# Mapped queries stored by the projections, a third bank for some maxima scores, two changed orders and a normalisation on ScalarE, in an infini-attention block with a gated feed-forward layer

## The chip, the cores and the metric

The kernel runs on one core of a Trainium2 chip. The metric is the device time of one execution in microseconds (us). Several engines of the core work side by side, each on its own sequence of instructions: TensorE (PE; its weight loads, PEld, are shown apart), VectorE (DVE), ScalarE (ACT), GpSimd (POOL), and SyncE (SP), which only issues transfers here. PSUM is the memory that TensorE writes its results into; the kernel divides it into banks of 128 x 512 fp32. SBUF is the memory for everything else on the core.

## The reference

A transformer block over 2048 tokens of width 576: attention with a compressive memory, then a gated feed-forward layer of width 4608, each after a layer normalisation that is scaled and shifted by a vector computed from a condition `c`. The attention has 32 heads of width 18 and goes through four segments of 512 tokens. Within a segment it is causal softmax attention; a memory matrix `M` and a normaliser `z` per head carry the segments before.

```python
mod = (_silu(c) @ w_mod).reshape(c.shape[0], 6, 1, -1)      # sa, ca, ga, sb, cb, gb
h = _layernorm(x) * (1 + ca) + sa
# attention: q, k, v = h @ wq, h @ wk, h @ wv, split in heads and segments
phi = lambda t: jnp.where(t > 0, t + 1.0, jnp.exp(t))
for s in range(N):
    logits = jnp.einsum("bhqd,bhkd->bhqk", qs, ks) * scale + mask
    p = _softmax(logits, axis=-1)
    a_dot = jnp.einsum("bhqk,bhkd->bhqd", p, vs)
    pq = phi(qs)
    num = jnp.einsum("bhld,bhde->bhle", pq, M)
    den = jnp.einsum("bhld,bhd->bhl", pq, z)[..., None] + 1e-6
    outs.append(g * num / den + (1.0 - g) * a_dot)
    pk = phi(ks)
    M = M + jnp.einsum("bhld,bhle->bhde", pk, vs)
    z = z + jnp.einsum("bhld->bhd", pk)
x = x + ga * (o @ wo)
h = _layernorm(x) * (1 + cb) + sb
x = x + gb * ((_silu(h @ w_gate) * (h @ w_up)) @ w_down)
```

All data is fp32.

## The kernel before

**Precision.** Products of fp32 matrices are made as three products of a high and a low part (`ah`, `al`, `dh`, `dl`, `wh`, `wl` and so on are such parts): high times high, high times low, low times high. A high part is made by a ScalarE copy that rounds, the low part by a VectorE subtraction.

**Projections.** Segment by segment (the loop `for s in range(NSEG)`), `proj(s, t)` makes nine tiles t of 128 rows of the q and k projections, transposed, 14 matmuls each (`mm14`, L100) into one of three PSUM banks tagged "p". Two ScalarE copies take a tile out of its bank (`fh`, `f`), a VectorE subtraction makes `fl`, and SP's queue stores the parts in DRAM (`kD`, `qD`). The order of the tiles is `QKORD`, 0 to 8: tiles 0 to 3 and half of 4 are k, the other half of 4 and tiles 5 to 8 are q. For segments above 0 the plain q rows are stored as well, in `qF`. `phi_k` maps the keys (a transpose by TensorE, minimum with 0, exponential, combine: L440 to L442), `vproj` makes v, `mem` adds to the memory matrix `mbd`. During segments 1 to 3 the generator `early()` makes the maxima of the first two units of the attention.

**Attention.** A unit u is four heads of one segment, so a segment s has eight units q = 0 to 7 and there are 32 in all. Every unit is a row of eleven steps, in an order written out by hand (`tc.manual_schedule()` keeps the instructions of each engine in the order of the program). In a step:
- `p2_step` makes the scores of unit u, keys by queries, in one of two PSUM banks tagged "s2" (L609), and ScalarE takes their exponential out of the bank (L612). GpSimd cuts off the part above the diagonal.
- `p1_step` makes scores of unit u + 2, queries by keys, in one of two banks "s1" (L184), of which VectorE takes the row maxima (L189). These are folded into the operand of that unit's `p2_step` through an extra row of `qst`. `p1_seq(u)` runs through all four row tiles of a unit.
- The events of the table `PAT` follow: one row of eleven strings for even and one for odd units of the first and of the second half of a segment. V: the product with v (L629); E, c, d: its way out of PSUM and its normalisation; A to D and G: reading the memory for the next segment with the mapped queries `pq` (L809); M, R, S, T, X, Z: the output projection of a segment that is done, whose accumulator is a single PSUM bank with the tag "w". Its first use is in unit 9 (`w = u - 9`). l, p, x: the layer normalisation behind it.
- The events f, g and h make the mapped queries of the next segment, row block t in the segment's unit q = t: f (one unit ahead; the call `event("f", -1)` before the loop makes the very first) loads the plain rows from `qF`; g runs three ScalarE passes, relu(-q), exp of its negative, relu(q) (L787 to L789); h adds two of them on GpSimd into `pq`.

The loads of a unit's operands (`load_stack`, four transfers) are issued three units ahead on SP's queue.

**Output projection of segment 3.** It runs after the attention, 8 groups of four steps n = 0 to 31. A group accumulates 14 matmuls (`wo_m`, L738) in one of two banks, and `wo_x` (L743) adds the result to the residual. The tuples `SS`, `HH` and `WW` say at which n the work for the following stage is woven in: sums of weight blocks (`sum_o`, L1161), sums of the operand (`y_here`), and with `WW` the first five weight pieces of the first pair (`prep_w`: a cast by ScalarE, L1175, and a subtraction by VectorE, L1176; with the first two also `prep_r`, the remainder rows).

**Feed-forward layer.** Tokens in two halves t, hidden columns in 18 pairs p. Gate (z = 0) and up (z = 1) are made with seven block products each, in the manner of Strassen and Winograd: `step(z, m)` runs product m with seven matmuls (`prod`, L1211) into a bank "A" (two of them), "B" or "C". Products 1, 6, 7 and 4 use A: 1 and 7 are added to by 6 and 4, and between the two a copy is taken (`copy_t`, L1240: `tb` after 6, `tc` after 7, in the very first set also `cu` after 1). `step` keeps the current A bank in `B["A"]`. The order of a pair's 14 products is `ZM`; the first set of all is taken in the order of indices `PRIME`. In the first half the generator `prep2` prepares the operand of the second half. It begins with the layer normalisation of five row tiles `xl` (L1078 to L1094), whose subtraction and scaling is the VectorE operation at L1092; the other tiles are normalised during the attention by GpSimd (L769) and ScalarE (L770).

Of the kernel before, what the change touches and what calls it, by code (L numbers as in the profile page):

```python
# [46 lines left out]
WW = (9, 11, 14, 18, 26)  # L47
# [7 lines left out]
PRIME = (0, 1, 3, 2, 5, 4) + tuple(range(6, 14))  # L55
# [5 lines left out]
PAT = (["", "M0", "V2 V3 m E D", "n", "M1 Q G", "c", "M2 d", "V0 g", "h A0 q M3 R S X", "T Y Z B0", "A1 P V1 z B1 f C"],  # L61
# [12 lines left out]
def block(ctx: ExitStack, tc: tile.TileContext, x, wqk, wv, wo, beta, wgu, wd, c, w_mod, wm01, out):  # L74
# [83 lines left out]
    mcol, pmt, mrow = {}, {}, {}  # L158

# [14 lines left out]
    def p1_step(u, b, i, ps, jp, jb):  # L174
# [6 lines left out]
        for h0 in range(0, 4, per):  # L181
            bank = ps.tile([P, L], F32, tag="s1", name="s1", bufs=S1B)
            for h in range(h0, h0 + per):
                nc.tensor.matmul(bank[:, n * (h - h0):n * (h - h0) + n],  # L184
                                 lhsT=qst[b][0:108, h, 128 * i:128 * i + 128],
                                 rhs=kst[b][0:108, h // 2, 0:n], start=True, stop=True)
            for h in range(h0, h0 + per):
                junk = jp.tile([P, L], BF16, tag="junk", name="junk", bufs=jb)
                nc.vector.tensor_tensor_reduce(junk[:, :n], bank[:, n * (h - h0):n * (h - h0) + n], tri[:, L - n:],  # L189
                                               1.0, -3e38, op0=ALU.add, op1=ALU.max, accum_out=mx[:, h, i:i + 1])  # L190
            if h0 + per < 4:
                yield
# [54 lines left out]
    with ExitStack() as p1:  # L247
# [211 lines left out]
        def proj(s, t):  # L459
# [16 lines left out]
            if q1 > 0:  # L476
# [4 lines left out]
                if s > 0:  # L481
                    nc.sync.dma_start(qF[s][q0:q1, :], f[r:])
# [108 lines left out]
    def p1_seq(u):  # L591
        if NE <= u < NU:
            for i in range(4):
                yield from p1_step(u, u % NB, 3 - i, ps, wk, 4)
# [182 lines left out]
    def phi_q(s, t):  # L777
        r = 64 if t == 0 else 0
        q0 = 0 if t == 0 else 64 + 128 * (t - 1)
        f = wk.tile([P, L], F32, tag="qf", name="qf", bufs=2)  # L780
        nc.sync.dma_start(f[r:], qF[s][q0:q0 + P - r, :])
        return f

    def phi_q2(s, t, f):
        r = 64 if t == 0 else 0
        e = wk.tile([P, L], F32, tag="qe", name="qe", bufs=1)
        nc.scalar.activation(e[r:], f[r:], AF.Relu, scale=-1.0)  # L787
        nc.scalar.activation(e[r:], e[r:], AF.Exp, scale=-1.0)
        nc.scalar.activation(f[r:], f[r:], AF.Relu)  # L789
        return e  # L790

    def phi_q3(s, t, f, e):
# [4 lines left out]
        nc.gpsimd.tensor_tensor(pqs[s][r:, t, :], e[r:], f[r:], op=ALU.add)  # L797
# [54 lines left out]
    def event(ev, u):  # L852
# [206 lines left out]
    def prep2(x2p):  # L1059
# [19 lines left out]
        for sn, i in ((2, 3), (3, 0), (3, 1), (3, 2), (3, 3)):  # L1079
# [10 lines left out]
            nc.gpsimd.tensor_tensor(rs, rs, mhalf[:, :1], op=ALU.pow)  # L1090
            yield
            nc.vector.tensor_scalar(xl, xl, mv[:, 0:1], rs[:, 0:1], op0=ALU.subtract, op1=ALU.mult)  # L1092
# [151 lines left out]
    def step(z, m):  # L1244
        prime = "set" not in B
        if m == 1:
            B["A"] = ps.tile([P, L], F32, tag="A", name="A", bufs=2)
# [3 lines left out]
        bank = B["B" if m == 2 else "C" if m in (5, 3) else "A"]  # L1251
# [104 lines left out]
    with tc.manual_schedule():  # L1356
# [4 lines left out]
        event("f", -1)  # L1361
# [291 lines left out]
```

## Time and profile before

| | us |
|---|---|
| device time, median of 3 runs | 1878.56 |
| lowest and highest run | 1877.34, 1879.14 |
| profiled execution, device time | 1879.11 |
| its span in the trace | 1877.4 |
| projections, from the start to the first step of the attention | 0 to 235 |
| attention, unit by unit | 235 to 594 |
| output projection of segment 3 | 594 to 612 |
| feed-forward layer | 612 to 1877 |

The borders of the stages are rounded to the microsecond. How the views of the profile are read:
- A row of busy time gives the engine, its busy us, the share of the span, and the number of instructions. Durations of matmuls overlap.
- A row of a group of instructions gives the line, the engine, the operation, output <- inputs with their shape, and the count; then busy us and mean ns of one; then the engine's idle time just before them and what ended most of it.
- A row of the timeline gives the start, the duration, the instruction, and in brackets how long the engine had been idle and what released it.
- A row of the waits gives the waiting instruction, what it waited for, and total us, times, and the longest.
- The chain of waits is followed back from the last instruction of a stretch, at each step to what released it, or else to the instruction before it on its engine.

### The profile page before, as it was taken

What the parts mean: (1) busy time and instruction counts of PE and PEld (TensorE: products, weight loads), DVE (VectorE), ACT (ScalarE), POOL (GpSimd) and SP (SyncE); (2) the same over time, 40 slices, a digit from 0 to 9 for tenths busy, and PEclk for the clock granted to TensorE, in tenths of its full rate; (3) what the DMA queues carried; (4) which work ended last, traced back from release to release, by engine and by line L of the source; (5) the groups of instructions that cost most, each with busy time, mean ns of one, the idle gap of its engine ahead of it and who ended that gap; (6) DMA issues with size and microseconds to landing.
All of it is one profiled execution on the core that took longest, in us unless ns stands there. A gap on an engine that the chain in (4) does not pass through costs nothing.

```text
span 1877.4 us, 30668 instructions
## 1 busy us (share of the span) xinstructions
PE 1855.3 (99%) x10933; PEld 1562.4 (83%) x10933; DVE 1487.8 (79%) x3282; ACT 978.4 (52%) x2138; POOL 507.8 (27%) x696
## 2 busy tenths in 40 slices
PE   8999999999999999999999999999999999999999
PEld 5988856777767788888888888888888888888888
DVE  7555278888886888888888888758888888888886
ACT  7433387768676534454544544434454454544442
POOL 2010046455565154454554454300000000000000
PEclk9999999999999999999999999999999999999999
DMA  8766644447655745555545534485333432333331
GB/s 299 248 224 239 221 146 146 144 141 197 170 161 211 248 160 193 164 169 186 186 153 169 168 125 150 151 286 186 104 102 100 125 103 87 115 104 124 101 101 53
DMA packets 177568, 303.42 MB, mean 162 GB/s; under 512 B 25960, under 2 KB 107496, under 8 KB 175496
## 3 DMA queue, kind: packets, MB, share of 16 engines
q1 hardware_dynamic: 150040, 246.48, 41.3%
q10 hardware_dynamic: 27376, 54.99, 8.3%
q8 instruction: 86, 1.41, 0.3%
q14 instruction: 66, 0.54, 0.1%
HBM read 187.53 MB, written 113.33 MB: 160 GB/s over the span
## 4 chain that ended last, share of the span: by engine, by line
PE 91%; DVE 4%; DMA 2%; ACT 2%; issue 1%; POOL 0%; SPq 0%; ACTq 0%; POOLq 0%; DVEq 0%
PE A L1211 23%; PE pd L1337 13%; PE C L1211 12%; PE pd L1320 10%; PE pp L100 6%; PE B L1211 6%; PE s L609 4%; PE s L184 4%; PE av L629 4%; PE pv L100 3%; PE pw L738 3%; DMA y<-yD 1%; DVE junk L189 1%; PE pn L809 1%; PE px L650 1%; PE pm L451 1%
## 5 line engine op out<-in xcount | busy, mean ns | idle before, releaser
L1211 PE MATMUL A<-y,wh 128*128 128x512 f32 x1152 | 406.4, 393 | 3.3 <-ACT tb L1240 1.3
L189 DVE CUSTOM_DVE_ANT_0 junk<-s,tri 128x256 bf16<-128x256 f32 (+3 forms) x512 | 227.6, 487 | 67.0 <-PE s L184 58.8
L1211 PEld LDWEIGHTS A<-y,wh 128*128 128x128 f32 x1152 | 216.8, 188 | 48.0 <-ACT tb L1240 2.2
L1176 DVE TENSOR_TENSOR wl<-O,wh 128x256 fp32r<-128x256 f32 x504 | 254.4, 510 | 0.7 <-ACT wh L1175 0.2
L1211 PE MATMUL A<-y,wl 128*128 128x512 f32 x576 | 227.0, 394 | 0.0
L612 ACT ACTIVATE Pt<-s 128x512 f32<-128x512 f32 (+1 forms) x352 | 186.7, 558 | 54.2 <-PE s L609 47.7
L1325 DVE TENSOR_TENSOR acc<-acc,pd 128x576 f32<-128x576 f32 x216 | 162.5, 752 | 58.6 <-PE pd L1320 51.9
L1211 PE MATMUL C<-y,wh 128*128 128x512 f32 x576 | 203.1, 393 | 0.3 <-DVE cu L1234 0.3
L1175 ACT CAST wh<-O 128x256 fp32r<-128x256 f32 x504 | 197.4, 405 | 0.9 <-DMA yD<-st 0.9
L1337 PE MATMUL pd<-dh,al 128*128 128x288 f32 x640 | 189.3, 296 | 0.0
L1337 PE MATMUL pd<-dh,ah 128*128 128x288 f32 x640 | 189.0, 295 | 0.0
L1337 PE MATMUL pd<-dl,ah 128*128 128x288 f32 x640 | 189.0, 295 | 0.0
L1166 POOL TENSOR_TENSOR O<-O 128x384 f32<-128x384 f32 x132 | 149.5, 1146 | 143.9 <-DMA O<-in_wgu_dram 37.3
L1341 DVE TENSOR_TENSOR acc<-acc,pd 128x576 f32<-128x576 f32 x156 | 116.8, 750 | 87.6 <-PE pd L1337 87.3
L1280 ACT CAST ah<-sg 128x512 fp32r<-128x512 f32 x192 | 119.1, 620 | 77.7 <-DVE sg L1235 71.4
L609 PE MATMUL s<-qs,ks 110*128 110x512 f32 (+2 forms) x384 | 148.7, 404 | 2.4 <-ACT Pt L612 1.9
L1281 DVE TENSOR_TENSOR al<-sg,ah 128x512 fp32r<-128x512 f32 x192 | 137.6, 716 | 9.6 <-ACT ah L1280 9.3
L184 PE MATMUL s<-ks,qs 108*128 108x256 f32 (+3 forms) x512 | 141.3, 329 | 1.1 <-DVE mx L189 0.2
L1320 PE MATMUL pd<-dh,ah 128*128 128x288 f32 x448 | 133.1, 297 | 0.0
L1320 PE MATMUL pd<-dh,al 128*128 128x288 f32 x448 | 132.6, 296 | 0.0
L1320 PE MATMUL pd<-dl,ah 128*128 128x288 f32 x448 | 132.5, 296 | 0.0
L1337 PEld LDWEIGHTS pd<-dl,ah 128*128 128x128 f32 x640 | 120.6, 188 | 7.1
(368 smaller groups left out, 4353.3 us busy)
## 6 DMA issues: line engine op xcount, KB each, us to landing
O<-in_wgu_dram SPq DMA_DIRECT2D x36, 768.0 KB
O<-oD SPq DMA_DIRECT2D x36, 512.0 KB
oD<-O ACTq DMA_DIRECT2D x34, 512.0 KB
ks<-kD SPq DMA_DIRECT2D x64, 216.0 KB
qs<-qD SPq DMA_DIRECT2D x64, 216.0 KB
O<-in_wgu_dram SPq DMA_DIRECT2D x36, 384.0 KB
rD<-wr ACTq DMA_DIRECT2D x36, 336.0 KB
wr<-rD SPq DMA_DIRECT2D x35, 336.0 KB
```

Source lines behind the costliest of these rows:

```text
L100: nc.tensor.matmul(ps, lhsT=a, rhs=b, start=(k == 0), stop=(k == 13))
L184: nc.tensor.matmul(bank[:, n * (h - h0):n * (h - h0) + n], lhsT=qst[b][0:108, h, 128 * i:128 * i + 128], rhs=kst[b][0:108, h // 2, 0:n], s ...
L189: nc.vector.tensor_tensor_reduce(junk[:, :n], bank[:, n * (h - h0):n * (h - h0) + n], tri[:, L - n:], 1.0, -3e38, op0=ALU.add, op1=ALU.max ...
L609: nc.tensor.matmul(bank[:, n * (g - h):n * (g - h + w)].rearrange("p (a b) -> p a b", a=w), lhsT=kst[u % NB][0:110, g // 2, 128 * j:128 * ...
L612: nc.scalar.activation(pt[:, h:h + per, :n], bank[:, :n * per].rearrange("p (a b) -> p a b", a=per), AF.Exp, scale=SCALE)
L1166: eng.tensor_tensor(o[:, d], o[:, a], o[:, b], op=op)
L1175: nc.scalar.copy(wh, o)
L1176: later.append(lambda: nc.vector.tensor_tensor(wl, o, f32(wh), op=ALU.subtract))
L1211: nc.tensor.matmul(bank, lhsT=a, rhs=b, start=(first and n == 0), stop=(n == 6), skip_group_check=not first)
L1320: nc.tensor.matmul(pd[:, i, :288], lhsT=a[:, tk], rhs=w, start=(k == 0), stop=(k == 2))
L1325: nc.vector.tensor_tensor(o, o, pd[:, :, :288], op=ALU.add)
L1337: nc.tensor.matmul(pd[:, i, :288], lhsT=a[:, tk], rhs=w, start=(k == 0), stop=(k == 5))
```

## The change

Five parts. Only the last, and the first on the projections' side, use other operations than before.

1. **Mapped q in the projections.** `proj` now maps the q rows of segments 1 to 3 itself (a minimum and a combine on VectorE, an exponential on ScalarE between them) and stores the mapped rows in `qF`. In the attention, `phi_q` loads them straight into the operand tile; the three ScalarE passes and the GpSimd addition are gone, and so is event g. Event f loads row block q + 1 in unit q, event h row block 0 in unit 0.
2. **A third bank for maxima scores.** For the maxima of the units below 11 (made in loop units 0 to 8) every third tile of `p1_step` goes into the bank "w", which the output projection does not use before unit 9.
3. **First set reordered.** In `PRIME` the product 1 of z = 1 comes before the product 4 of z = 0. Since two A banks are then open, `step` keeps one for each z.
4. **First weight pieces later.** In `WW` the first two pieces of weight preparation go from steps 9 and 11 to 11 and 13, the third from 14 to 15.
5. **ScalarE normalises.** In `prep2` GpSimd makes -mean * rstd, and ScalarE scales and shifts the row tile, which VectorE did.

```diff
-WW = (9, 11, 14, 18, 26)
+WW = (11, 13, 15, 18, 26)
...
-PRIME = (0, 1, 3, 2, 5, 4) + tuple(range(6, 14))
+PRIME = (0, 1, 3, 2, 5, 4, 7, 6) + tuple(range(8, 14))
...
-    def p1_step(u, b, i, ps, jp, jb):
+    def p1_step(u, b, i, ps, jp, jb, spare=0):
...
         for h0 in range(0, 4, per):
-            bank = ps.tile([P, L], F32, tag="s1", name="s1", bufs=S1B)
+            turn[0] += 1
+            if spare and turn[0] % 3 == 0:
+                bank = ps.tile([P, L], F32, tag="w", name="s1", bufs=spare)
+            else:
+                bank = ps.tile([P, L], F32, tag="s1", name="s1", bufs=S1B)
...
                 if s > 0:
-                    nc.sync.dma_start(qF[s][q0:q1, :], f[r:])
+                    e = pb.tile([P, L], F32, tag="pq1", name="pq1")
+                    nc.vector.tensor_scalar(e[r:], f[r:], 0.0, None, op0=ALU.min)
+                    nc.scalar.activation(e[r:], e[r:], AF.Exp)
+                    nc.vector.scalar_tensor_tensor(e[r:], f[r:], 0.0, e[r:], op0=ALU.max, op1=ALU.add)
+                    nc.sync.dma_start(qF[s][q0:q1, :], e[r:])
...
-                yield from p1_step(u, u % NB, 3 - i, ps, wk, 4)
+                yield from p1_step(u, u % NB, 3 - i, ps, wk, 4, WB if u < 11 else 0)
...
     def phi_q(s, t):
-        r = 64 if t == 0 else 0
-        q0 = 0 if t == 0 else 64 + 128 * (t - 1)
-        f = wk.tile([P, L], F32, tag="qf", name="qf", bufs=2)
-        nc.sync.dma_start(f[r:], qF[s][q0:q0 + P - r, :])
-        return f
-
-    def phi_q2(s, t, f):
-        r = 64 if t == 0 else 0
-        e = wk.tile([P, L], F32, tag="qe", name="qe", bufs=1)
-        nc.scalar.activation(e[r:], f[r:], AF.Relu, scale=-1.0)
-        nc.scalar.activation(e[r:], e[r:], AF.Exp, scale=-1.0)
-        nc.scalar.activation(f[r:], f[r:], AF.Relu)
-        return e
-
-    def phi_q3(s, t, f, e):
         if t == 0:
             pqs[s] = sk2.tile([P, 5, L], F32, tag="pq", name=f"pq{s}")
             nc.gpsimd.memset(pqs[s][0:64, 0, :], 0.0)
         r = 64 if t == 0 else 0
-        nc.gpsimd.tensor_tensor(pqs[s][r:, t, :], e[r:], f[r:], op=ALU.add)
+        q0 = 0 if t == 0 else 64 + 128 * (t - 1)
+        nc.sync.dma_start(pqs[s][r:, t, :], qF[s][q0:q0 + P - r, :])
...
-        elif n == "f":
-            sn, qn = divmod(u + 1, 8)
-            if u + 1 < NU and sn < 3 and qn < 5:
-                fq[u + 1] = phi_q(sn + 1, qn)
-        elif n in "gh" and s < 3 and q < 5:
-            if n == "g":
-                fq[-2] = phi_q2(s + 1, q, fq[u])
-            else:
-                phi_q3(s + 1, q, fq.pop(u), fq[-2])
+        elif n == "f" and s < 3 and q < 4:
+            phi_q(s + 1, q + 1)
+        elif n == "h" and s < 3 and q == 0:
+            phi_q(s + 1, 0)
...
+            nb = x2p.tile([P, 1], F32, tag="nb3", name="nb")
+            nc.gpsimd.tensor_scalar(nb, mv[:, 0:1], rs[:, 0:1], -1.0, op0=ALU.mult, op1=ALU.mult)
             yield
-            nc.vector.tensor_scalar(xl, xl, mv[:, 0:1], rs[:, 0:1], op0=ALU.subtract, op1=ALU.mult)
+            nc.scalar.activation(xl, xl, AF.Identity, scale=rs[:, 0:1], bias=nb[:, 0:1])
...
         if m == 1:
-            B["A"] = ps.tile([P, L], F32, tag="A", name="A", bufs=2)
+            B["A", z] = ps.tile([P, L], F32, tag="A", name="A", bufs=2)
...
-        bank = B["B" if m == 2 else "C" if m in (5, 3) else "A"]
+        bank = B["B"] if m == 2 else B["C"] if m in (5, 3) else B["A", z]
...
-        event("f", -1)
```

In `PAT` the event g is taken out of its four places.

More of the change, by code (lines that the diff above doesn't have):

```diff
@@ L60 @@
 E2 = 2
-PAT = (["", "M0", "V2 V3 m E D", "n", "M1 Q G", "c", "M2 d", "V0 g", "h A0 q M3 R S X", "T Y Z B0", "A1 P V1 z B1 f C"],
[1 row of a table removed]
+PAT = (["", "M0", "V2 V3 m E D", "n", "M1 Q G", "c", "M2 d", "V0", "h A0 q M3 R S X", "T Y Z B0", "A1 P V1 z B1 f C"],
[1 row of a table added]
        ["", "M0", "V2 V3 m E", "", "D G M1 c n", "", "Q V0 d g R", "h", "M2 q M3 A0 S B0 X", "Z Y", "P f z V1 A1 T B1 C"],
[1 row of a table removed]
[1 row of a table added]
 LNA = 1
@@ L158, in block @@
     mcol, pmt, mrow = {}, {}, {}
+    turn = [0]
     def load_stack(u, b):
```

4 rows, old and new, of the table PAT are left out of this document.

## The prediction

> **What bounds the kernel now.** I read the page's first and fourth parts first, then the time cut into stages, then the waits stage by stage.
>
> ```profile
> PE 1855.3 (99%) x10933; PEld 1562.4 (83%) x10933; DVE 1487.8 (79%) x3282; ACT 978.4 (52%) x2138; POOL 507.8 (27%) x696
> PE 91%; DVE 4%; DMA 2%; ACT 2%; issue 1%; POOL 0%; SPq 0%; ACTq 0%; POOLq 0%; DVEq 0%
> ```
>
> TensorE sets the end: 91% of the chain that ended last is its matmuls. The change touches no matmul, so it can only win time in which TensorE waits: at most the 9% of 1877.4 us that the chain spends elsewhere, some 170 us, and only at the places touched. A busy share of 99% hides waits, since the recorded durations of matmuls overlap; so I look at waits, and at starts of one matmul after another. By stages (columns: TensorE, its weight loads, VectorE, ScalarE, GpSimd, each busy us and count, then clock, DMA share, GB/s):
>
> ```profile
> 74.00:98.00 24.00, 24.00 (x121) 19.66 (x120) 22.69 (x67) 9.71 (x19) 2.20 (x6) 1.00 0.80 262
> 98.00:122.00 24.00, 24.00 (x149) 21.87 (x148) 12.42 (x41) 6.62 (x17) 1.17 (x3) 1.00 0.65 229
> 135.00:190.00 55.00, 54.93 (x353) 48.73 (x352) 30.82 (x68) 21.10 (x40) 5.48 (x10) 1.00 0.69 238
> 190.00:235.00 45.00, 45.00 (x243) 38.95 (x242) 7.75 (x12) 17.64 (x33) 0.51 (x1) 1.00 0.67 232
> 235.00:320.00 85.00, 82.72 (x570) 51.40 (x568) 70.88 (x293) 66.69 (x136) 47.93 (x88) 1.00 0.48 148
> 320.00:594.00 274.00, 271.11 (x2048) 196.11 (x2048) 218.66 (x888) 202.75 (x422) 153.02 (x296) 1.00 0.54 156
> ```
>
> The first four rows are the projections of segments 1, 2 and 3, the fifth is attention units 0 to 8, the sixth the other units. The clock is full throughout. In units 0 to 8 all three engines are near their limits (TensorE 97%, VectorE 83%, ScalarE 78%): there waits can be won. In the projections TensorE alone is full, except that VectorE has 1.3 us left of 24 in the first row.
>
> **The change part by part.** Each term is time off the path, against the profiled execution's own 1879.1 us.
>
> *Third bank for the maxima scores, units 0 to 8.* The waits of the weight loads in 235 to 320 us (total, times, longest), then the chain of that stretch:
>
> ```profile
> PEld s L609 <- ACT Pt L612: 15.5, 27, 0.9
> PEld s L184 <- DVE mx L189: 3.8, 14, 0.5
> PEld s L609 <- ACT qe L787: 2.5, 3, 0.8
> by line: PE s L609 21.1%; PE s L184 20.4%; PE av L629 17.8%; DVE junk L189 7.6%; ACT Pt L612 6.4%; PE pn L809 5.2%; PE px L650 3.6%; DVE r L659 3.0%; issue 2.6%; ACT avs L641 2.4%; DVE o L663 1.6%; DVE wol L921 1.6%; PE pmt L203 1.0%; ACT n
> 240.82 0.64 ACT qe L787
> 241.48 0.63 ACT qe L788
> 242.11 0.52 ACT qf L789
> ```
>
> A maxima score (L184) may start when VectorE has reduced the score two tiles back; with three banks it is three tiles back. A reduction of a 512-wide tile takes 0.69 us, one of 384 0.55, an exponential (the other half of each pair of matmuls) 0.60 and 0.49:
>
> ```profile
> L189 DVE CUSTOM_DVE_ANT_0 junk<-s,tri 128x512 bf16<-128x512 f32 x36 | 23.8, 686 | 19.8 <-PE s L184 18.6 <-POOL ml L196 0.6 <-POOL Pt L616 0.6
> L189 DVE CUSTOM_DVE_ANT_0 junk<-s,tri 128x384 bf16<-128x384 f32 x32 | 17.2, 553 | 2.8 <-PE s L184 2.2
> L612 ACT ACTIVATE Pt<-s 128x512 f32<-128x512 f32 x60 | 33.9, 597 | 7.2 <-PE s L609 3.6 <-POOL mc L194 2.2
> L612 ACT ACTIVATE Pt<-s 128x384 f32<-128x384 f32 x32 | 15.2, 489 | 3.6 <-PE s L609 3.2
> ```
>
> So VectorE is the slower partner by under 0.1 us a pair; what the spare bank mostly absorbs is VectorE's side jobs, which come in one piece. The gain lies between nothing (the score for the exponentials still has two banks, and ScalarE's 15.5 us of waits take over) and 6.5 us, VectorE's 7.6% of the chain's 85 us on this line. I take 3.0, near the row of 3.8 us which is the wait itself. What is late next is the exponential.
>
> *Mapped q made in the projections; the attention side loses it.* Away go 15 times three ScalarE passes (the last three chain rows: 1.8 us on the chain in unit 0) and 15 GpSimd additions. In unit 0 the three passes stand ahead of an exponential that TensorE waits for; the other four sets of units 0 to 7 are not on the chain. Between 0 and 5 x 1.8 = 9.0 us; I take 1.5, as the row on the chain is 1.8. In units 8 to 23 ScalarE is 74% busy, and the same wait is
>
> ```profile
> PEld s L609 <- ACT qe L787: 3.4, 4, 0.8
> ```
>
> Such a load wait was there also behind other names, and is mostly covered by the running matmuls: 0 to 3.4, taken as 0.5. The loads of the mapped rows now go straight into the operand tile. Their number on SP's queue stays 15; the first of each segment moves behind the four stack loads issued in its unit, the others follow the same position. The last row block is loaded in the segment's fourth unit and first read in its fifth, about 10 us later, so nothing waits. The zeroing of 64 rows by GpSimd stays.
>
> *The projection side gains* 15 times: a minimum and a combine on VectorE, an exponential on ScalarE between them; the store of mapped q now waits for VectorE. Nearest rows, from the same map for keys (the minimum there reads PSUM; one that reads SBUF is L231):
>
> ```profile
> L440 DVE TENSOR_SCALAR pe<-ptk 128x512 f32<-128x512 f32 x8 | 5.4, 672 | 0.0
> L442 DVE SCALAR_TENSOR_TENSOR pk<-ptk,pe 128x512 f32<-128x512 f32 x8 | 5.5, 689 | 1.0 <-ACT pe L441 0.9
> L441 ACT ACTIVATE pe<-pe 128x512 f32<-128x512 f32 x8 | 5.1, 634 | 8.7 <-DVE pe L440 8.7
> L231 DVE TENSOR_SCALAR x<-x,mv,rs 128x576 f32<-128x576 f32 x8 | 4.1, 575 | 0.0
> ```
>
> Per tile 0.58 to 0.67 + 0.69 = 1.27 to 1.36 us of VectorE and 0.63 of ScalarE; per segment of five tiles 6.3 to 6.8 and 3.2. In segment 1 the q tiles fall mainly into 98 to 122 us, where VectorE has 24.0 - 12.4 = 11.6 us free; segments 2 and 3 have 24 and 37 us free. The cover is TensorE's own work. The new wait is ScalarE's, for the minimum: behind it in ScalarE's queue stand the next tile's two copies out of PSUM, for which TensorE waits only when all three projection banks are full. On SP the stores of the next tile stand behind the later store; nobody reads them soon. If the cover failed in segment 1 alone, it would cost up to 6.8; a gain is excluded, as nothing is removed there. I take a loss of 0.5.
>
> *First weight pieces later.* The output projection of segment 3 has a hole:
>
> ```profile
> 604.42 0.37 PE L738 MATMUL pw<-woh,oh 128*128 128x288 f32 x1 [0.88 <-DVE xr L743]
> 602.20 1.25 DVE L1161 TENSOR_TENSOR wr<-O,wr 32x384 fp32r<-32x384 f32 x1
> 603.48 0.43 DVE L1176 TENSOR_TENSOR wl<-O,wh 128x256 fp32r<-128x256 f32 x1
> 603.82 0.45 DVE L743 TENSOR_TENSOR xr<-pw,xr 128x288 f32<-128x288 f32 x1
> ```
>
> TensorE waits for a PSUM bank that the residual addition (603.82) must empty, and that stood behind two pieces of weight preparation. With the first piece at step 11 instead of 9 the built order puts the addition ahead of both: it can start about 602.2, and the 0.88 us goes. The next addition then stands behind the two and a y subtraction; its bank is wanted a group of 14 matmuls later (1.9 us), so up to 0.9 could come back. Between 0 and 0.9; I take 0.9. The pieces themselves are wanted at 612.25, some 6 us later.
>
> *First set reordered.* TensorE waits because product 4 of the first operand accumulates into the bank that ScalarE is still copying:
>
> ```profile
> 619.87 0.39 PE L1211 MATMUL A<-y,wh 128*128 128x512 f32 x1
> 620.10 0.39 PE L1211 MATMUL A<-y,wr 96*128 96x512 f32 x1
> 621.16 0.50 PE L1211 MATMUL A<-y,wh 128*128 128x512 f32 x1 [0.67 <-ACT tc L1240]
> 620.52 0.58 ACT L1240 COPY tc<-A 128x512 f32<-128x512 f32 x1 [1.56 <-PE A L1211]
> 618.39 0.55 DVE L1161 TENSOR_TENSOR wr<-O,wr 32x384 fp32r<-32x384 f32 x1
> 622.20 0.68 DVE L1161 TENSOR_TENSOR wr<-O,wr 32x512 fp32r<-32x512 f32 x1
> ```
>
> Back to back matmuls start 0.23 us apart (619.87, 620.10), so the next product would start at 620.33; it starts at 621.16: 0.83 us lost. Product 1 of the second operand, in the other A bank, now runs there (7 x 0.23 = 1.6 us), and the copy is over by 621.10. It needs the remainder rows' first three slices, ready at 618.94. Gain 0.8, less if a later wait is only moved.
>
> *ScalarE normalises* five row tiles in the first feed-forward pairs: one VectorE operation becomes one of ScalarE (the nearest: L770) and a GpSimd multiplication (0.27, L769).
>
> ```profile
> L1092 DVE TENSOR_SCALAR ha<-ha,mv,rs x5: 574/770/1679, 656.9 to 735.0; 128x576 f32<-128x576 f32 x5
> L770 ACT ACTIVATE xh<-xr,nb,rs x11: 863/870/874, 354.1 to 586.0; 128x576 f32<-128x576 f32 x11
> L769 POOL TENSOR_SCALAR nb<-mv,rs x11: 263/265/270, 353.7 to 584.3; 128x1 f32<-128x1 f32 x11
> 675.76 1.66 DVE L1176 TENSOR_TENSOR wl<-O,wh 128x256 fp32r<-128x256 f32 x1
> 675.63 1.50 POOL L1189 TENSOR_TENSOR dr__9450<-dr__9450,gbB 128x576 f32<-128x576 f32 x1
> 679.37 0.50 PE L1211 MATMUL A<-y,wh 128*128 128x512 f32 x1 [1.33 <-ACT tb L1240]
> ```
>
> The only wait of TensorE above 0.5 us near these five is at 679.37, and comes from a VectorE subtraction stretched to 1.66 us (0.43 at 603.48) beside a GpSimd multiplication, before the normalisation. It stays. New on ScalarE: the normalisation waits for GpSimd, with a weight cast and a bank copy behind it. Bounds: 5 x 0.87 = 4.4 lost, if each lands ahead of a copy that TensorE waits for, to 1.3 won; taken as 0, as ScalarE is idle half of the time.
>
> [...]
>
> **Sum**: -3.0 - 1.5 - 0.5 - 0.9 - 0.8 + 0.5 + 0 = -6.2: 1879.1 - 6.2 = **1872.9 us**. The runs' median, 1878.56, is 0.5 below the profiled execution, within their spread of 1.8.
>
> **Rivals.**
> - *ScalarE takes the wait over.* The third bank gains nothing, because the exponentials' two banks end every wait. For it: 15.5 us against 3.8. Against it: VectorE's line has more of the chain than ScalarE's, 7.6% to 6.4%. Time: 1872.9 + 3.0 = 1875.9.
> - *More than its own waits.* The whole 6.5 us of VectorE's line, and the waits put down to the first of the three passes (2.5 and 3.4 us) with the 1.8 on the chain: 6.5 + 1.8 + 2.5 + 3.4 + 0.9 + 0.8 = 15.9, so 1863.2. Against it: TensorE's own work stands beside most of those waits.
> - *Slower: the projections become VectorE's.* From 74 to 98 us VectorE is 95% busy. If its lag at the q tiles of segments 1 and 2 exceeds two tile times (2 x 3.3 us, as 14 matmuls take), ScalarE's exponential holds the copies, the three banks fill, and each tile costs its 1.36 us: 10 x 1.36 = 13.6, so 1886.5. It decides from that lag on; against it stand the 11.6 and 24 us free.
> - *The moved product doesn't run early.* It waits for the whole remainder tile (622.20 + 0.68 = 622.88, where its seventh matmul is due at 620.33 + 6 x 0.23 = 621.7): the 0.8 is lost and 1.2 paid, 1874.9. Against it: slices, not tiles, carry the order in the built program.
>
> **Chances.** Forecast 0.55; ScalarE takes over 0.22; more 0.09; slower 0.08; product not early 0.06. Some 0.2% (3.8 us, below 1874.8) is what a measurement can tell from no change. Faster: most of the forecast (0.47), all of "more" (0.09), a part of the others (0.08), 0.64; slower 0.08; within 0.2% the rest, 0.28. The range 1867.0 to 1878.5 holds the forecast with its bounds, the takeover and the unready product, and leaves out the slower case and the far end of "more". Most chance has one sign.
>
> **What would show it.** In units 0 to 8: waits of L184 on VectorE's maxima from 3.8 to about 1 us, the stretch shorter by some 4.5 us, and the exponentials first among the waits. In the projections: no wait of TensorE for ScalarE's copies, and the first exponential at the same time as before to 0.5 us. At the output projection no 0.88 us hole; in the first set no wait for `tc`; the 1.33 us wait for `tb` still there. I am wrong if the score matmuls' waits merely change their releaser, or if attention starts more than 2 us late.

## The result, and the profile after

| | median, us | runs | lowest to highest |
|---|---|---|---|
| before | 1878.93 | 10 | 1877.34 to 1880.29 |
| changed | 1874.03 | 10 | 1872.62 to 1875.96 |

The ratio is 0.9975, with a 95% interval of 0.9966 to 0.9985: 4.9 us faster. The span of the profiled execution went from 1877.4 to 1872.2 us. A second set of runs of the changed kernel, among the experiments below, gave 1873.58 us and 0.9971 (0.9960 to 0.9983). One execution of one kernel below, the one with other steps for the weight pieces, took 4982.27 us and is left out of its median.

The page of the changed kernel, its parts on busy time and on the chain that ended last:

```profile
PE 1851.9 (99%) x10933; PEld 1560.2 (83%) x10933; DVE 1493.6 (80%) x3307; ACT 969.0 (52%) x2113; POOL 490.9 (26%) x686
PE 93%; DVE 3%; DMA 2%; ACT 1%; issue 1%; POOL 0%; SPq 0%; ACTq 0%; POOLq 0%; DVEq 0%
```

The count of matmuls is the same. Their share of the chain rose from 91 to 93%, while VectorE's and ScalarE's fell by a point each: the time came out of waits. Where it came out is seen best from the starts of single matmuls that are the same in both traces (the first score matmul of a unit, the last matmul of the output projection, the first of a set of 14 products). Each row below is the length of a stretch, in us:

| stretch | before | changed | difference | forecast |
|---|---|---|---|---|
| start to the first score of unit 0 | 235.26 | 235.44 | +0.18 | +0.5 |
| unit 0 to unit 9 | 91.26 | 88.47 | -2.79 | -3.0 bank, -1.5 mapped q |
| unit 9 to unit 31 | 254.26 | 254.44 | +0.18 | -0.5 |
| unit 31 to the end of the output projection | 31.33 | 30.98 | -0.35 | -0.9 |
| to the first product | 0.14 | 0.13 | -0.01 | |
| first set of products | 24.31 | 23.23 | -1.08 | -0.8 |
| second set | 36.47 | 36.48 | +0.01 | |
| third set | 37.05 | 35.50 | -1.55 | 0 (ScalarE normalises) |
| the rest, to the last matmul | 1162.97 | 1163.15 | +0.18 | |
| sum | 1873.06 | 1867.83 | -5.23 | -6.2 |

A set is the 14 products of a pair, 98 matmuls, with what the down projection runs between them. The sum was nearly met because a term that was too large (the attention) and one that was missed (the third set) stood against each other.

The waits of the weight loads in units 0 to 8 (235 to 320 us) of the changed kernel:

```profile
PEld s L618 <- ACT Pt L621: 19.6, 38, 1.1
PEld av L638 <- issue: 2.2, 7, 0.4
PEld pmt L208 <- issue: 1.4, 7, 0.2
...
PEld s L618 <- ACT nm L813: 1.0, 1, 1.0
```

The maxima scores (now L189) wait for VectorE no more: before there were 3.8 us of it. The scores for the exponentials (L618) wait longer for ScalarE than before, 19.6 against 15.5 us. In the chain of waits of the same stretch a new member stands fourth:

```profile
by line: PE s L618 29.1%; PE av L638 22.3%; PE s L189 20.8%; DMA qs<-mr 7.1%; ACT Pt L621 5.2%; PE pn L804 4.7%; PE px L659 4.1%; ACT avs L650 2.4%; issue 1.1%; PE pmt L208 1.0%; DVE r L668 0.8%; PE pv L100 0.8%; DVE junk L194 0.7%; ACT nm 
```

VectorE's reductions fell from 7.6 to 0.7% of the chain and ScalarE's three passes are off it. But 7.1% are now one transfer, `qs<-mr`: the row of maxima that the first score of a unit needs in its operand. The timeline of TensorE shows the place, the first score of unit 7, and the chain shows the transfer from its issue on:

```profile
297.69 6.03 DMA qs<-mr
303.85 0.47 PE s L618
```
```profile
303.85 0.47 PE L618 MATMUL s<-qs,ks 110*128 110x512 f32 x1 [0.81 <-DMA qs<-mr]
```

The queue of SP in the changed kernel shows what stands ahead of that row:

```profile
293.91 0.36 SPq L903 DMA_DIRECT2D woraw<-in_wo_dram  x1
294.37 0.29 SPq L167 DMA_DIRECT2D ks<-kD  x1
295.03 0.29 SPq L168 DMA_DIRECT2D qs<-qD  x1
295.38 0.33 SPq L167 DMA_DIRECT2D ks<-kD  x1
295.75 0.34 SPq L168 DMA_DIRECT2D qs<-qD  x1
297.13 1.23 SPq L173 DMA_DIRECT2D qs<-mr  x2
```

A piece of the output weights and the four operand loads of unit 9 are issued in the 3.2 us before it.

### The profile page after: what moved, and what is told of

Read it like the earlier page. It is cut to its first block, busy times and chain, and to the rows that moved or that the text cites. A ratio compares the mean times of both kernels' runs of the same rounds, so it can differ in the third digit from the quotient of the medians.

```text
span 1872.2 us, 30685 instructions
## 1 busy us (share of the span) xinstructions
PE 1851.9 (99%) x10933; PEld 1560.2 (83%) x10933; DVE 1493.6 (80%) x3307; ACT 969.0 (52%) x2113; POOL 490.9 (26%) x686
## 4 chain that ended last, share of the span: by engine, by line
PE 93%; DVE 3%; DMA 2%; ACT 1%; issue 1%; POOL 0%; SPq 0%; ACTq 0%; POOLq 0%; DVEq 0%
PE A L1203 24%; PE pd L1329 13%; PE C L1203 12%; PE pd L1312 10%; PE pp L100 6%; PE B L1203 6%; PE s L618 4%; PE av L638 4%; PE s L189 4%; PE pv L100 3%; PE pw L747 3%; PE pn L804 1%; DMA y<-yD 1%; DVE junk L194 1%; PE px L659 1%; PE pm L456 1%
## 5 line engine op out<-in xcount | busy, mean ns | idle before, releaser
L1168 DVE TENSOR_TENSOR wl<-O,wh 128x256 fp32r<-128x256 f32 x504 | 244.8, 491 | 2.1 <-ACT wh L1167 1.6
L618 PE MATMUL s<-qs,ks 110*128 110x512 f32 (+2 forms) x384 | 149.0, 405 | 2.7 <-ACT Pt L621 1.5
L189 PE MATMUL s<-ks,qs 108*128 108x256 f32 (+3 forms) x512 | 139.6, 324 | 0.8 <-DVE mx L194 0.2
```

The lines of the kernel that those rows point to most:

```text
L189: nc.tensor.matmul(bank[:, n * (h - h0):n * (h - h0) + n], lhsT=qst[b][0:108, h, 128 * i:128 * i + 128], rhs=kst[b][0:108, h // 2, 0:n], s ...
L618: nc.tensor.matmul(bank[:, n * (g - h):n * (g - h + w)].rearrange("p (a b) -> p a b", a=w), lhsT=kst[u % NB][0:110, g // 2, 128 * j:128 * ...
L1168: later.append(lambda: nc.vector.tensor_tensor(wl, o, f32(wh), op=ALU.subtract))
```

## The experiments

Each was timed beside the kernel before on one chip, and its ratio is to that partner. First the parts alone, each put into the kernel before.

**Third bank alone.**
```diff
 (before)
+            turn[0] += 1
+            if spare and turn[0] % 3 == 0:
+                bank = ps.tile([P, L], F32, tag="w", name="s1", bufs=spare)
+            else:
                 bank = ps.tile([P, L], F32, tag="s1", name="s1", bufs=S1B)
...
+                yield from p1_step(u, u % NB, 3 - i, ps, wk, 4, WB if u < 11 else 0)
```


> Before with the third bank for the maxima scores of units 0 to 8 alone. The stretch from the first score of unit 0 to that of unit 9 is 91.26 us before and 88.48 in the changed kernel, 2.8 less. Theory (the bank wins most of it): about 2.0 less here, so 89.3, and the waits of the maxima scores for VectorE, 3.8 us before, are gone. Rival (the mapped queries won it, the bank only swaps one wait for another): the same waits are gone, but the waits of the other scores for ScalarE grow by as much, and the stretch is shorter by under 0.7 us. Nothing else in the kernel moves, and the wait for the copy tb in the third pair (1.33 us) stays. Time: 1876.9 by the theory, 1878.3 by the rival.

1876.86 us, ratio 0.9989 (0.9980 to 0.9998). Unit 0 to unit 9 took 88.96 us, 2.30 less than before. The waits of its weight loads in that stretch:

```profile
PEld s L614 <- ACT Pt L617: 19.4, 37, 1.1
PEld s L614 <- ACT qe L792: 1.7, 2, 0.8
```

The maxima scores' 3.8 us are gone. The other scores' waits grew by as much (15.5 to 19.4), as the rival said, and still the stretch is 2.3 us shorter. Before, the three rows of such waits that the prediction shows come to 21.8 us, while TensorE had a matmul running in 82.72 of the 85 us: for the most part these waits are covered by matmuls that still run. So their sum is no measure of time lost; the stretch is.

**Mapped queries alone.** The parts of the diff in `proj`, `phi_q`, the events and `PAT`.
```diff
 (before)
-                    nc.sync.dma_start(qF[s][q0:q1, :], f[r:])
+                    e = pb.tile([P, L], F32, tag="pq1", name="pq1")
...
+                    nc.sync.dma_start(qF[s][q0:q1, :], e[r:])
...
-            if n == "g":
-                fq[-2] = phi_q2(s + 1, q, fq[u])
```


> Before with the mapped queries made in the projections alone. Theory: the attention starts 0.2 us later (235.44), the stretch from unit 0 to unit 9 is 0.8 us shorter, mainly in unit 0, and from unit 9 on nothing is won (the changed kernel had 254.4 us from unit 9 to unit 31, before 254.3). Rival (the mapped queries carry the gain): the stretch is 2.0 or more shorter with the waits of the maxima scores for VectorE still there. Time: 1878.3 by the theory, 1877 by the rival.

1879.30 us, ratio 1.0000 (0.9991 to 1.0009): nothing. Unit 0 to unit 9 took 91.65 us, 0.39 longer than before. Unit 0 was 0.32 shorter and unit 2 0.13, but unit 6 took 11.60 instead of 10.59, for the same reason as in the changed kernel:

```profile
306.32 0.47 PE L613 MATMUL s<-qs,ks 110*128 110x512 f32 x1 [0.72 <-DMA qs<-mr]
```

**The two orders alone.**
```diff
 (before)
-WW = (9, 11, 14, 18, 26)
+WW = (11, 13, 15, 18, 26)
-PRIME = (0, 1, 3, 2, 5, 4) + tuple(range(6, 14))
+PRIME = (0, 1, 3, 2, 5, 4, 7, 6) + tuple(range(8, 14))
```


> Before with the two changed orders alone: later weight pieces, and the first set reordered. Theory: the output projection of segment 3 ends 0.4 us earlier (a wait of 0.7 for the residual addition stays, one group later), the first set takes 1.1 us less, and the wait for the copy tb in the third pair, 1.33 us before, stays, since the normalisation is the old one. Rival (that wait went because the time at which the pair begins had moved against GpSimd's work): it is gone here too, and 1.5 us more are won. Time: 1877.4 by the theory, 1875.9 by the rival.

1878.04 us, ratio 0.9991 (0.9982 to 0.9999). From unit 31 to the end of the output projection 0.36 less, in the first set 1.09 less; the wait for `tb` in the third pair of sets was still there:

```profile
678.41 0.50 PE L1211 MATMUL A<-y,wh 128*128 128x512 f32 x1 [1.05 <-ACT tb L1240]
```

**ScalarE normalises, alone.**
```diff
 (before)
+            nb = x2p.tile([P, 1], F32, tag="nb3", name="nb")
+            nc.gpsimd.tensor_scalar(nb, mv[:, 0:1], rs[:, 0:1], -1.0, op0=ALU.mult, op1=ALU.mult)
             yield
-            nc.vector.tensor_scalar(xl, xl, mv[:, 0:1], rs[:, 0:1], op0=ALU.subtract, op1=ALU.mult)
+            nc.scalar.activation(xl, xl, AF.Identity, scale=rs[:, 0:1], bias=nb[:, 0:1])
```


> Before with the normalisation on ScalarE alone. Theory: the wait for the copy tb in the third pair is gone (1.5 us between matmuls), since GpSimd's new small operation pushes its large multiplication past the VectorE operation that the copy waits for; the rest stays. Rival (the move of the pair's begin did it): the wait stays, and the time is that of before. Time: 1877.4 by the theory, 1878.9 by the rival.

1878.03 us, ratio 0.9994 (0.9985 to 1.0002). The third set took 35.45 us instead of 37.05, and TensorE had no wait there. The wait that is gone was not the same in every kernel: in before and the three parts above it lasted from 0.87 to 1.33 us, and the third set took 36.58 to 37.05 us. So 1.1 to 1.6 us belong to this part.

**GpSimd's small multiplication alone.** The result `nb` is not used; the normalisation stays on VectorE.
```diff
 (before)
+            nb = x2p.tile([P, 1], F32, tag="nb3", name="nb")
+            nc.gpsimd.tensor_scalar(nb, mv[:, 0:1], rs[:, 0:1], -1.0, op0=ALU.mult, op1=ALU.mult)
             yield
             nc.vector.tensor_scalar(xl, xl, mv[:, 0:1], rs[:, 0:1], op0=ALU.subtract, op1=ALU.mult)
```


> Before with GpSimd's new small multiplication alone: its result is not used, VectorE normalises as before. Theory (what removed the wait for tb is that GpSimd's large multiplication begins a microsecond later, past the VectorE operation on which the copy tb waits; the normalisation itself stood behind that operation in VectorE's queue and had no part in it): the wait is gone, the third set takes 35.5 us as with the whole part (35.45) instead of 37.05. Rival (VectorE relieved of the normalisation): the wait of 1.3 us and the 37 us stay. Time: 1877.6 by the theory, 1878.9 by the rival.

1877.76 us, ratio 0.9992 (0.9983 to 1.0001). The third set took 35.44 us: the same gain without taking any work off VectorE. The timeline of this kernel, GpSimd, then VectorE, then ScalarE:

```profile
675.14 1.08 POOL L1092 TENSOR_SCALAR nb<-mv,rs 128x1 f32<-128x1 f32 x1
676.18 1.43 POOL L1191 TENSOR_TENSOR dr__9454<-dr__9454,gbB 128x576 f32<-128x576 f32 x1
...
676.09 0.68 DVE L1236 TENSOR_TENSOR cu<-C,tb 128x512 f32<-128x512 f32 x1
676.81 1.35 DVE L1237 TENSOR_TENSOR sg<-cu,sg 128x512 f32<-128x512 f32 x1
...
678.09 0.57 DVE L1094 TENSOR_SCALAR ha<-ha,mv,rs 128x576 f32<-128x576 f32 x1
...
676.88 0.59 ACT L1242 COPY tb<-A 128x512 f32<-128x512 f32 x1 [1.75 <-DVE cu L1236]
```

The copy `tb` may start when `cu` has read the old `tb`. In the kernel before GpSimd's 1.5 us multiplication ran just ahead of `cu` and stretched a VectorE subtraction in front of it to 1.66 us. Now it starts a microsecond later: `cu` is done at 676.77, and the operation that is stretched (to 1.35 us) is the one behind, for which TensorE does not wait. The normalisation stands behind both.

The two stretched operations (1.66 us before and 1.35 here, against 0.43 and 0.69 undisturbed) have both inputs in SBUF, while `cu`, with one input in PSUM, took 0.68 us here, 0.59 of it beside the same multiplication. What slows them is not shown beyond this. GpSimd's own small operation is not always short either: here it took the 1.08 us of the row above, and the five of the changed kernel took from 0.27 to 1.08 us.

The others start from the changed kernel.

**Operand loads behind the maxima row, in unit 6.**
```diff
 (changed kernel)
-            load_unit(u + 3)
+            if u != 6:
+                load_unit(u + 3)
...
+                if u == 6 and k == 4:
+                    load_unit(u + 3)
```


> The changed kernel with one move: in unit 6 the four operand loads are issued after the maxima row of the next unit instead of before it. Theory (the row's two small transfers queue behind the loads): they land within 3 us of their issue instead of 6.0 to 6.4, the first score of unit 7 no longer waits for them, unit 6 takes 10.1 us instead of 11.12, and unit 0 to unit 9 take 87.5 instead of 88.47. Rival (the row is late for another reason): the transfers still take about 6 us and unit 6 stays at 11.1. What could go wrong is that the loads themselves are late for unit 7, by up to 3 us. Time: 1873.0 by the theory, 1874.0 by the rival.

1877.90 us, ratio 0.9995 (0.9986 to 1.0004): most of the gain is lost. The row's transfers now landed 1.8 and 2.1 us after their issue, and unit 6 took 10.04 us instead of 11.12: that it had queued behind the loads holds. But the loads came too late for the maxima scores of unit 9, in unit 7, which took 16.64 us:

```profile
305.93 0.47 PE L189 MATMUL s<-ks,qs 108*128 108x512 f32 x1 [2.38 <-DMA ks<-kD]
307.68 0.77 PE L189 MATMUL s<-ks,qs 108*128 108x512 f32 x1 [1.05 <-DMA qs<-qD]
```

The two holes are 3.4 us; the rest of the loss is the granted clock behind them, 0.50 from 307.48 to 314.30 us. Four windows there (columns: TensorE, weight loads, VectorE, ScalarE, GpSimd, then clock, DMA share, GB/s):

```profile
307.00:309.00 2.00, 1.32 (x3) 1.17 (x4) 0.65 (x3) 0.35 (x2) 0.00 (x0) 0.62 0.60 198
309.00:311.00 2.00, 2.00 (x15) 0.80 (x18) 1.74 (x7) 1.10 (x2) 0.54 (x3) 0.50 0.59 156
311.00:313.00 2.00, 2.00 (x18) 1.62 (x11) 0.40 (x1) 1.21 (x3) 1.61 (x3) 0.50 0.56 167
313.00:315.00 2.00, 2.00 (x11) 1.97 (x11) 0.58 (x3) 0.64 (x2) 0.00 (x0) 0.67 0.11 30
```

**Other steps for the weight pieces.**
```diff
 (changed kernel)
-WW = (11, 13, 15, 18, 26)
+WW = (11, 17, 20, 22, 26)
```


> The changed kernel with the weight pieces at steps 11, 17, 20, 22 and 26 instead of 11, 13, 15, 18 and 26. Theory (the 0.7 us wait for the residual addition at step 16 came back because two pieces stand ahead of that addition): the wait is gone, and the output projection of segment 3 takes 16.1 us from its first to its last matmul instead of 16.78, unless a later addition is held up by 0.2 to 0.5. Rival (GpSimd's or the copies' lateness holds the addition): the wait stays and it takes 16.8. Time: 1873.4 by the theory, 1874.0 by the rival.

1874.79 us, ratio 0.9973 (0.9962 to 0.9983): as the changed kernel. The wait for the residual addition moved on by another group and shrank, and the output projection took 16.44 us from its first to its last matmul instead of 16.78. The pieces that are later now made the first set 0.41 us longer, at its end:

```profile
604.57 0.37 PE L747 MATMUL pw<-woh,oh 128*128 128x288 f32 x1 [0.50 <-DVE xr L752]
```
```profile
632.00 0.50 PE L1203 MATMUL C<-y,wh 128*128 128x512 f32 x1 [0.90 <-DVE cu L1226]
```

The attention of this kernel is that of the changed one, and yet unit 6 took 10.51 us instead of 11.12, and unit 0 to unit 9 87.89 instead of 88.47. Its first score of unit 7 hardly waited for the maxima row:

```profile
303.03 0.47 PE L618 MATMUL s<-qs,ks 110*128 110x512 f32 x1 [0.23 <-DMA qs<-mr]
```

**The spare bank for the other scores.**
```diff
 (changed kernel)
-                yield from p1_step(u, u % NB, 3 - i, ps, wk, 4, WB if u < 11 else 0)
+                yield from p1_step(u, u % NB, 3 - i, ps, wk, 4)
...
+            turn[0] += 1
+            if u < 9 and turn[0] % 3 == 0:
+                bank = ps.tile([P, L], F32, tag="w", name="s2", bufs=WB)
+            else:
                 bank = ps.tile([P, L], F32, tag="s2", name="s2", bufs=S2B)
```


> The changed kernel with the spare bank given to the other scores: in units 0 to 8 every third score tile for the exponentials goes into the bank w, the maxima scores keep two. Theory (VectorE is the slower of the two partners, and the exponentials' waits are mostly the time of the exponential itself): the waits of the maxima scores for VectorE are back (about 4 us), those of the other scores fall below the 19.6 us of the changed kernel by at most half, and unit 0 to unit 9 take 89.5 to 91 us instead of 88.47. Rival (ScalarE's two banks have been the bound, and a bank is worth as much or more there): 88.5 or less. Time: 1875.5 by the theory, at most 1874 by the rival.

1876.13 us, ratio 0.9982 (0.9973 to 0.9991). Unit 0 to unit 9 took 90.18 us, 1.7 more than with the bank on the maxima. The waits:

```profile
PEld s L188 <- DVE mx L193: 11.4, 26, 0.8
PEld s L621 <- ACT Pt L624: 9.8, 13, 0.8
```

The waits for ScalarE fell by half, those for VectorE came back threefold (11.4 where about 4 was expected). VectorE was the slower partner, and the bank belongs where it was put.

**The changed kernel again, and a two by two of mapped queries and earlier output weights.** First the changed kernel as it is.


> The changed kernel once more, as the partner of the next three. Theory (the wait of unit 7's first score for the maxima row is a transfer that lands at the edge): unit 6 takes between 10.1 and 11.2 us, unit 0 to unit 9 87.5 to 88.5. Rival (the wait belongs to the change in every execution): 11.1 and 88.5 again. The other units, the output projection and the first three sets are those of the first profile to 0.1 us. Time: 1874.5.

1873.58 us, ratio 0.9971 (0.9960 to 0.9983). Unit 6 took 11.14 us, unit 0 to unit 9 88.49: the wait of unit 7 came again, as the rival said. That it belongs to every execution is not shown: with the other weight steps, and the same code in the attention, unit 6 took 10.51.

```diff
 (changed kernel)
-WQ = (0, 3, 4, 5, 6)
+WQ = (0, 1, 2, 3, 4)
```


> The changed kernel with the five pieces of the output weights loaded and prepared in units 0 to 4 instead of 0 and 3 to 6 (the operations are the same). Theory (the load of such a piece, which waits in SP's queue for VectorE, stands ahead of the four operand loads, and these ahead of the maxima row): the row's transfers in unit 6 land within 4 us of their issue instead of 6.0 to 6.4, unit 6 takes 10.1 us, unit 0 to unit 9 87.5. Rival (the operand loads alone make it late): the transfers still take 5 us or more, and unit 6 varies between 10.1 and 11.2. What could go wrong is that the preparation, now in units 1 to 5, holds up ScalarE or VectorE there, by up to 0.3 us a unit. Time: 1873.5 by the theory, 1874.5 by the rival.

1875.28 us, ratio 0.9982 (0.9973 to 0.9991). In unit 6 the row landed within 2.3 us and the unit took 10.03 us, as expected. But units 2, 3 and 4 took 9.89, 11.07 and 11.37 us instead of 9.52, 9.39 and 10.09. The waits of TensorE from 260 to 290 us, then its matmul at the start of unit 4 and the windows from there:

```profile
PE s L618 <- DMA qs<-mr: 2.0, 2, 1.7
```
```profile
274.06 0.47 PE L618 MATMUL s<-qs,ks 110*128 110x512 f32 x1 [1.69 <-DMA qs<-mr]
```
```profile
274.00:276.00 2.00, 1.95 (x6) 1.17 (x6) 1.21 (x3) 1.08 (x2) 0.00 (x0) 0.72 0.71 199
276.00:278.00 2.00, 2.00 (x20) 0.73 (x18) 0.83 (x4) 0.60 (x1) 0.00 (x0) 0.50 0.64 203
278.00:280.00 2.00, 2.00 (x13) 1.86 (x12) 1.15 (x4) 1.87 (x5) 0.71 (x2) 0.92 0.57 186
```

The same wait for the same row has moved to the units where the weights' loads are now, next to those of the mapped queries. There it is longer, and behind it the granted clock was 0.50 for 3.4 us besides.

```diff
 (changed kernel)
-                    e = pb.tile([P, L], F32, tag="pq1", name="pq1")
...
-                    nc.sync.dma_start(qF[s][q0:q1, :], e[r:])
+                    nc.sync.dma_start(qF[s][q0:q1, :], f[r:])
```
with the events f, g and h of before:


> The changed kernel without the mapped queries (they are made in the attention again, as before). Theory (with the third bank there the three ScalarE passes are the next to hold up units 0 and 2): unit 0 takes 9.5 instead of 8.8 us, unit 2 10.0 instead of 9.5, unit 0 to unit 9 88.9, and the later units are the same to 0.3 us; the attention begins at the same time to 0.4 us. Rival (beside the bank the mapped queries are worth nothing, or cost the wait of unit 7): unit 0 to unit 9 88.0 or less. Time: 1875.2 by the theory, 1874.0 by the rival.

1874.57 us, ratio 0.9977 (0.9968 to 0.9986). Unit 0 took 9.55 us instead of 8.80 in its partner, unit 2 9.97 instead of 9.53, unit 6 10.38 instead of 11.14; unit 0 to unit 9 89.04. From unit 9 to unit 31 it took 254.13, the partner 254.40. So beside the third bank the mapped queries won 0.55 us net in units 0 to 8; by the device time the two kernels can't be told apart, as the intervals of their ratios overlap.

```diff
 (changed kernel without the mapped queries)
-WQ = (0, 3, 4, 5, 6)
+WQ = (0, 1, 2, 3, 4)
```


> The same without the mapped queries, and with the output weights loaded in units 0 to 4. Theory: unit 0 and unit 2 as without the mapped queries, unit 6 at 10.1, unit 0 to unit 9 88.7; the gain from the earlier loads is smaller than beside the mapped queries (0.2 against up to 1.0), since the row just came in time there. Rival: the earlier preparation meets the three ScalarE passes in the same units and costs 0.5 or more. Time: 1875.0 by the theory, 1875.7 by the rival.

1876.66 us, ratio 0.9989 (0.9980 to 0.9998). Units 0 and 2 as expected (9.55 and 9.97), unit 6 10.03; but unit 3 took 11.40 us, and unit 0 to unit 9 90.86. TensorE's waits from 255 to 290 us show why, and it is not the three passes:

```profile
PE s L614 <- DMA qs<-mr: 1.8, 1, 1.8
```

So the late row comes with the earlier loads of the weights, with and without the mapped queries. Here it made unit 3 2.0 us longer; beside the mapped queries units 2 to 4 grew by 3.3 us, with the lower clock in it.

None of these kernels was measured faster than the changed one.

## Why the prediction was right, and where its steps were not

The time of 1874.03 lies 1.1 us above the forecast. By its own steps:

- **Third bank, forecast -3.0: right in kind, a little large.** Alone it gave -2.30. The waits it was to remove went from 3.8 to nothing, the exponentials came first among the waits, as said. The rival that ScalarE takes the wait over was right about the waits (15.5 to 19.4 us) and wrong about the time; the spare bank on ScalarE's side, with all else the same, gave a stretch 1.7 us longer.
- **Mapped queries in the attention, forecast -1.5 and -0.5: right in kind, given back at a place that the prediction did not look at.** Beside the third bank units 0 and 2 won 0.75 and 0.44 us, together 1.19 of the 1.5. But unit 6 lost 0.76, and the net was -0.55 (89.04 to 88.49). Alone the part lost 0.39. The step that failed is that of the loads ("so nothing waits"): it asked who waits for the mapped rows, and not which transfer of the same queue has no slack. In the kernel before, the maxima row for unit 7 landed 0.20 us before its first score, by the completions in the trace; a score that waits for the row starts 0.13 us behind its landing, so there was next to no margin. A shorter unit alone doesn't make the wait of 0.8 us, though: with the third bank and without the mapped queries it was 0.04 and 0.10 us. In five kernels with the mapped queries and the loads in their old place it was 0.81, 0.85, 0.72, 0.23 and 0.00 us, the longer ones where the operand loads ahead of the row landed later. The later term of 0.5 was not there at all: units 9 to 31 took 254.26 before, 254.44 after, and 254.13 with the queries mapped in the attention again. The 3.4 us of waits that it was taken from are gone, but those for the exponential grew by 2.8 us: for the most part the waits only changed what ended them. From 320 to 594 us, before and after:

```profile
PEld s L609 <- ACT Pt L612: 17.0, 32, 0.9
```
```profile
PEld s L618 <- ACT Pt L621: 19.8, 34, 0.9
```

- **Projections, forecast +0.5 within 0 to 6.8: right.** The attention began 0.18 us later; kernels with unchanged projections began it between 235.24 and 236.05, so no loss can be told from none. VectorE had the room that was read off, and the operations were cheaper than their nearest rows: the minimum took 0.42 us, not 0.58 to 0.67, so 1.11 us a tile. From 98 to 122 us, and the two VectorE rows (q tiles of 128 rows):

```profile
98.00:122.00 24.00, 24.00 (x149) 21.80 (x148) 17.26 (x51) 9.39 (x21) 1.23 (x3) 1.00 0.65 230
```
```profile
L490 DVE SCALAR_TENSOR_TENSOR pq<-pf,pq 128x512 f32<-128x512 f32 x12 | 8.3, 691 | 4.4 <-ACT pq L489 4.4
L488 DVE TENSOR_SCALAR pq<-pf 128x512 f32<-128x512 f32 x12 | 5.1, 422 | 0.0
```

- **Weight pieces, forecast -0.9: mis-sized, -0.36.** The hole at step 12 is gone. What the prediction named as its bound ("up to 0.9 could come back") came back in the main: the next addition now stands behind both pieces. In the changed kernel, TensorE and then VectorE:

```profile
603.68 0.40 PE L747 MATMUL pw<-woh,oh 128*128 128x288 f32 x1 [0.71 <-DVE xr L752]
```
```profile
602.12 0.68 DVE L1153 TENSOR_TENSOR wr<-O,wr 32x512 fp32r<-32x512 f32 x1
602.84 0.43 DVE L1168 TENSOR_TENSOR wl<-O,wh 128x256 fp32r<-128x256 f32 x1
603.18 0.45 DVE L752 TENSOR_TENSOR xr<-pw,xr 128x288 f32<-128x288 f32 x1
```

- **First set, forecast -0.8: right, -1.08.** The hole of 0.83 us is gone. The matmuls behind it also start a little closer (7 in 1.65 us, now in 1.61), and 0.1 went into the longer wait at the set's end. That the moved product would find its operands was right too.
- **ScalarE normalises, forecast 0: wrong, -1.55 in these two traces, and 1.1 to 1.6 by the kernels with and without this part.** The step that failed is "It stays": the prediction found the cause of the 1.33 us wait (GpSimd's multiplication beside VectorE), and did not ask when that multiplication would start once a new operation stood ahead of it in GpSimd's own queue. The experiment with the small multiplication alone gave the whole gain. In one kernel with this part, that of the later operand loads, 0.37 us of the wait stayed and the set took 36.10 us. ScalarE's 0.87 us a tile cost nothing visible, and VectorE's relief was worth nothing either: the gain came from a shift in time. With GpSimd's small multiplication in both, the third set took 35.45 us with the normalisation on ScalarE and 35.44 with it on VectorE.

So the mechanism of the larger part was right (TensorE waits for VectorE's maxima), the total came near, and two terms were off in opposite directions: of the 5.0 us forecast for the bank and the queries in the attention 2.6 came (2.79 less the 0.18 of units 9 to 31), and 1.55 came unforeseen. That these two nearly cancel is luck.

**Left open:** why in three kernels with the mapped queries the operand loads of unit 9, issued in unit 6, land later. By the completions in the traces the row's second transfer took 6.03, 6.05 and 6.13 us in three kernels with the mapped queries, but 5.12 and 5.41 in two others with them (the spare bank on the other side, the other weight steps), and 4.92 to 5.28 in six without. In all eleven it landed 0.36 to 0.44 us behind the last of those loads. The transfers issued in that unit are the same and of the same size, and no run here shows the cause.

## What to carry to other kernels

A small transfer with a consumer at once can share its queue's fate with the bulk loads issued just ahead of it: here it landed 0.4 us behind the last of them, 6.03 us after its issue in the changed kernel, and with the loads issued behind it 1.8 and 2.1 us after its issue. Before a stretch is made shorter, look up how long before its use each such transfer lands (here 0.20 us). Moving bulk loads is no cure by itself: in the three kernels that did it, it moved the wait to another unit and made it dearer (holes of 1.69, 1.82 and 2.38 us; the changed kernel had 0.81). And an operation added to an idle engine can win time by shifting what that engine does next, against an engine whose operations run longer beside it: here the added operation delayed a GpSimd multiplication beside which a VectorE subtraction had taken 1.66 us instead of 0.43, and the third set took 35.44 us instead of 37.05.

## What was not expected of the hardware

After some holes TensorE's granted clock fell to 0.50: behind the 1.69 us hole at the start of unit 4 with the earlier output weights for 3.4 us, and in the run with the later operand loads for 6.8 us behind holes of 2.38 and 1.05 us. The length of the hole alone doesn't decide: a hole of 1.82 us at the start of unit 4 (earlier output weights, without the mapped queries) had a clock of 1.00 behind it, and with the mapped queries alone a hole of 1.96 us in the feed-forward layer left it at 1.00:

```profile
1262.06 0.47 PE L1196 MATMUL A<-y,wh 128*128 128x512 f32 x1 [1.96 <-DMA y<-yD]
```
```profile
1262.00:1264.00 2.00, 1.94 (x9) 1.66 (x10) 0.00 (x0) 0.04 (x1) 0.00 (x0) 1.00 0.98 310
1264.00:1266.00 2.00, 2.00 (x15) 1.90 (x14) 0.45 (x1) 0.85 (x2) 0.00 (x0) 1.00 1.08 276
```

What decides whether the clock falls is not shown by these runs.

The wait before the second half of the tokens (1.96 us in the row above) was 0.6 us before and in the changed kernel, 1.0 with the two orders alone and 1.8 with the other steps for the weight pieces; the feed-forward rest took from 1161.96 to 1164.46 us in the traces with all but the same code.
